# K^T and V^T of each attention head by DMA transposes in place of TensorE transposes

## The chip, the cores and the metric

The kernel runs on one core of a Trainium2 chip. The metric is device time in microseconds (us), the median of several executions. A core has TensorE (PE in the profile; its weight loads are PEld), VectorE (DVE), ScalarE (ACT), GpSimd (POOL) and SyncE (SP). In this kernel SP issues all DMA transposes, and POOL issues the ordinary loads and stores of the attention stage.

## The reference

Forward and backward pass of an attention block over a given K and V cache, multiplied by a gated branch. Cut to what the change touches (x is 2048 x 576, 32 heads of 128, 2048 keys, all bf16):

```python
q      = (xn @ wq).reshape(B, Sq, H, Dh).transpose(0, 2, 1, 3)
scores = einsum("bhqd,bhkd->bhqk", q, k_cache) * Dh ** -0.5
p      = softmax(scores)
o      = einsum("bhqk,bhkd->bhqd", p, v_cache)
s      = o.transpose(0, 2, 1, 3).reshape(B, Sq, H * Dh) @ wo
out    = x + s * silu(gated(xn))      # and the gradients of everything, by jax.vjp
```

The backward pass needs `dP = dO V^T` and `dQ = dS K`. So each head uses K and V in two forms: as they lie (keys on the partitions) for `P V` and `dS K`, and transposed (head dimension on the partitions) for `Q K^T` and `dO V^T`.

## The kernel before

Each head has two halves of 16 slots, one for each block of 128 queries. In the first half a slot makes `sp = Q K^T` and `Pq = exp(sp)`; in the second `dp = dO V^T`, and `Pq` becomes dS. Each finished 128 x 2048 slab of `Pq` (512 KB) is turned by a DMA transpose on SP's queue, into `PT` or `dST`, and TensorE reads that five slots later (`SKEW`), as weights of the "tail" matmuls. So 32 slabs per head already went through the DMA transpose.

```python
def pe_transpose_blocks(src_fn, lo, hi, dst_fn, eng):
    for g in range(lo, hi, 8):
        n = min(8, hi - g)
        pt = acc_tile(bf)
        for j in range(n):
            nc.tensor.transpose(pt[:, j, :], src_fn(g + j), ident[:])
        alt.copy(dst_fn(g, n), pt[:, :n, :], eng=eng)
...
def prep_kt(hs):      # 16 TensorE transposes, two ACT copies out of PSUM
    KTv = hs.KT[:].rearrange("p (t q) -> p t q", q=P)
    pe_transpose_blocks(lambda j: hs.Kn[:, j, :], 0, NT, lambda g, n: KTv[:, g:g + n, :], "s")

def prep_vt(hs):      # 16 TensorE transposes, two DVE copies out of PSUM
    VTv = hs.VT[:].rearrange("p (t q) -> p t q", q=P)
    pe_transpose_blocks(lambda j: hs.Vn[:, j, :], 0, NT, lambda g, n: VTv[:, g:g + n, :], "v")
...
def transpose_slab(hs, qt, name):
    T = wpt.tile([P, NT, P], bf, name=name, tag="PT")        # 7 buffers for PT and dST together
    nc.sync.dma_start_transpose(T[:], hs.slabs[qt][:])
    return T
...
def tail_part(hs, T, rhs, part):
    ...
    for kt in range(part * NT // 2, (part + 1) * NT // 2):
        nc.tensor.matmul(hs.acc[:, 0, :], lhsT=T[:, kt, :], rhs=rhs[:, kt, :], start=(kt == 0), stop=(kt == NT - 1))
...
def plan(h):                                   # put(slot, TensorE columns, work)
    b1, b2 = 2 * NT * h, 2 * NT * h + NT       # first and second half
    pl = b2 - 2 * NT if h else None            # second half of the head before
    if h:
        ...
        for c in range(4):
            put(pl + q(c), 0, lambda c=c: load_k(hd(), c, 4))
            put(pl + q(skew + 3 + c), 0, lambda c=c: load_v(hd(), c, 4))
        ...
        put(pl + q(skew + 3), NT * P, lambda: prep_kt(hd()))
    ...
    put(b1 + q(NSC + 2), NT * P, lambda: prep_vt(hd()))
```

KT and VT have one buffer each, Kn has two, Vn has one. The slot in `put` gives the order in which work is recorded; a scheduler then moves an instruction earlier on its engine's queue when it expects it to be ready.

Of the kernel before, what the change touches and what calls it, by code (L numbers as in the profile page):

```python
# [13 lines left out]
P = 128  # L14
# [52 lines left out]
def kernel(  # L67
# [6 lines left out]
    nc = tc.nc  # L74
# [6 lines left out]
    NT = S // P  # L81
# [59 lines left out]
# [7 lines that stand above are left out]
# [4 lines left out]
    def new_head(h):  # L152
        hs = HeadState()
        hs.h = h
        hs.wq, hs.woT = wqs[h % 2], woTs[h % 2]
        hs.Kn = Kns[h % 2]
        hs.Vn, hs.VT, hs.KT, hs.QT, hs.dOT, hs.dOn, hs.Qn = Vn, VT, KT, QT, dOT, dOn, Qn
        return hs

    def load_wq(hs):  # L160
        hcols = slice(hs.h * P, (hs.h + 1) * P)
        nf = DT - 1 if KPAD else DT
        if nf:
            nc.gpsimd.dma_start(hs.wq[:, :nf, :], A_wq[:nf * P, hcols].rearrange("(i p) c -> p i c", p=P))
        if KPAD:
            nc.gpsimd.dma_start(hs.wq[LO:, nf, :], A_wq[nf * P:, hcols])

    def load_wo(hs):
        nf = (DT - 1) * P if KPAD else D
        rows = slice(hs.h * P, (hs.h + 1) * P)  # L170
        if nf:
            nc.gpsimd.dma_start(wo_h[:, :nf], A_wo[rows, :nf])
        if KPAD:
            nc.gpsimd.dma_start(wo_h[:, nf + LO:], A_wo[rows, nf:])
# [5 lines left out]
    def load_k(hs, c=0, n=1):  # L180
        load_kv(hs, hs.Kn, A_k_cache, c, n)

    def load_v(hs, c=0, n=1):
        load_kv(hs, hs.Vn, A_v_cache, c, n)
# [9 lines left out]
    def prep_kt(hs):  # L194
        KTv = hs.KT[:].rearrange("p (t q) -> p t q", q=P)
        pe_transpose_blocks(lambda j: hs.Kn[:, j, :], 0, NT, lambda g, n: KTv[:, g:g + n, :], "s")

    def prep_vt(hs):
        VTv = hs.VT[:].rearrange("p (t q) -> p t q", q=P)
        pe_transpose_blocks(lambda j: hs.Vn[:, j, :], 0, NT, lambda g, n: VTv[:, g:g + n, :], "v")  # L200

    def prep_wot(hs):
        pt = acc_tile(bf)
        for i in range(DT):
            nc.tensor.transpose(pt[:, i, :], wo_h[:, i * P:(i + 1) * P], ident[:])
        alt.copy(hs.woT[:], pt[:, :DT, :], eng="s")
# [9 lines left out]
    def prep_qt(hs, sc):  # L216
        gen_T(hs.wq, xnT, hs.QT, sc, "s")

    def prep_dot(hs, sc):
        gen_T(hs.woT, dsT, hs.dOT, sc, "v")  # L220

    def prep_don(hs, sc):
        pe_transpose_blocks(lambda j: hs.dOT[:, j * P:(j + 1) * P], sc * nb, (sc + 1) * nb,
                            lambda g, n: hs.dOn[:, g:g + n, :], "v")

    def prep_qn(hs):
        pe_transpose_blocks(lambda j: hs.QT[:, j * P:(j + 1) * P], 0, NT, lambda g, n: hs.Qn[:, g:g + n, :], "v")
# [359 lines left out]
    NSC = S // CH  # L587
    nb = CH // P

    def attention(fast):  # L590
        with ExitStack() as es:
# [9 lines left out]
            skew = min(SKEW if fast else 2, NT // 2)  # L601
# [4 lines left out]
                return ps_acc.tile([P, 8, P], bf, name="acct", tag="acc")  # L606
            acc_box[0] = acc_alloc

            def start_head(h):
                hs = heads_pre[h] if h == 0 else new_head(h)  # L610
                hs.rs_all = hstat.tile([P, NT], f32, name="rs_all")
                hs.rinv_all = hstat.tile([P, NT], f32, name="rinv_all")
                hs.negdelta = hstat.tile([P, NT], f32, name="negdelta")
                hs.rsc = hstat.tile([P, NT], f32, name="rsc")
                hs.slabs = [None] * NT
                hs.PT = [None] * NT
                hs.dST = [None] * NT
                return hs
# [41 lines left out]
            def scale_don(hs, qt):  # L660
                nc.vector.tensor_scalar(hs.dOn[:, qt, :], hs.dOn[:, qt, :], hs.rinv_all[:, qt:qt + 1], None, op0=ALU.mult)

            def scale_qn(hs, qt):
                nc.vector.tensor_scalar(hs.Qn[:, qt, :], hs.Qn[:, qt, :], hs.rinv_all[:, qt:qt + 1], None, op0=ALU.mult)
# [12 lines left out]
            def tail1(hs, qt, part):  # L677
                tail_part(hs, hs.PT[qt], hs.Vn, part)
                if part == 0:
                    return  # L680
                hs.PT[qt] = None
                op_ = hs.acc
                if qt % G4 == 0:
                    hs.o_n = stg.tile([P, G4, P], bf, name="o_n")
                alt.scaled(hs.o_n[:, qt % G4, :], op_[:, 0, :], hs.rinv_all[:, qt:qt + 1], eng=("s" if qt >= NT - skew else "v"))
                junk = wt.tile([P, P], f32, name="junk")
                nc.vector.scalar_tensor_tensor(junk[:], op_[:, 0, :], -1.0, hs.dOn[:, qt, :], op0=ALU.mult, op1=ALU.mult,  # L687
                                               accum_out=hs.negdelta[:, qt:qt + 1])
                store_nat(hs, hs.o_n, qt, on2_d)

            def post1(hs):
                nc.vector.tensor_scalar(hs.rsc[:], hs.rinv_all[:], SCALE, None, op0=ALU.mult)
# [57 lines left out]
            def part_tile():  # L750
                return stg.tile([P, NT, P], f32, name="part", tag="part", bufs=1)
# [4 lines left out]
            def put(slot, cols, fn):  # L756
                units.setdefault(slot, []).append((cols, fn))
# [18 lines left out]
            def q(k):  # L776
                return min(k, NT - 1)

            def plan(h):
                b1, b2 = 2 * NT * h, 2 * NT * h + NT  # L780
                hd = lambda: heads[h]
                pl = b2 - 2 * NT if h else None
                if h:
                    put(pl, 0, lambda: heads.__setitem__(h, start_head(h)))
                    for c in range(4):
                        put(pl + q(c), 0, lambda c=c: load_k(hd(), c, 4))
                        put(pl + q(skew + 3 + c), 0, lambda c=c: load_v(hd(), c, 4))
                    put(pl + q(4), 0, lambda: load_wo(hd()))
                    put(pl + q(5), 0, lambda: load_wq(hd()))
                    put(pl + q(skew + 3), NT * P, lambda: prep_kt(hd()))  # L790
                    put(pl + q(skew + 4), DT * P, lambda: prep_wot(hd()))
                    for sc in range(NSC):
                        put(pl + q(skew + 4 + 2 * sc), DT * CH, lambda sc=sc: prep_qt(hd(), sc))
                for qt in range(NT):
                    put(b1 + qt + skew, NT * P // 2, lambda qt=qt: tail1(hd(), qt, 0))
                    put(b1 + qt + skew, NT * P // 2, lambda qt=qt: tail1(hd(), qt, 1))
                for sc in range(NSC):
                    put(b1 + q(sc), DT * CH, lambda sc=sc: prep_dot(hd(), sc))
                    put(b1 + q(sc + 1), nb * P, lambda sc=sc: prep_don(hd(), sc))
                for qt in range(NT):  # L800
                    put(b1 + max(qt + 1, q(2 + qt // nb)), 0, lambda qt=qt: scale_don(hd(), qt))
                put(b1 + q(NSC + 2), NT * P, lambda: prep_vt(hd()))
                put(b1 + q(NTH + 2), NT * P, lambda: prep_qn(hd()))
                for qt in range(NT):
                    put(max(b1 + qt + 1, b1 + NT - 4 + qt // 2 if qt < NTH else b1 + NT + qt), 0, lambda qt=qt: scale_qn(hd(), qt))
                put(b2 + 1, 0, lambda: post1(hd()))
                parts = {}

                def first(key, rhs, lo, hi, eng, factor=1.0):
                    parts[key] = part_tile()  # L810
                    return Partial(hd(), lo, hi, rhs, parts[key], None, eng, factor)
                spread(b1 + NTH, lambda: first("v", hd().dOn, 0, NTH, "v"))
                spread(b2, lambda: Partial(hd(), NTH, NT, hd().dOn, parts["v"], out_3[0, h], None))
                spread(b2 + NTH, lambda: first("k", hd().Qn, 0, NTH, "s", SCALE))
                spread(b2 + NT, lambda: Partial(hd(), NTH, NT, hd().Qn, parts["k"], out_2[0, h], None, SCALE))
                for qt in range(NT):
                    put(b2 + qt + skew, NT * P // 2, lambda qt=qt: tail2(hd(), qt, 0))
                    put(b2 + qt + skew, NT * P // 2, lambda qt=qt: tail2(hd(), qt, 1))
# [386 lines left out]
```

## Time and profile before

| | |
|---|---|
| median of 3 runs | 5043.2 us (5036.47 to 5043.98) |
| attention stage (first sp to last dp matmul) | 490 to 3633 us: 3142 us |
| busy in it | PE 3074 us (98%), ACT 2129 us (68%), DVE 1988 us (63%) |
| one head, from its first sp matmul to that of the next | 97.68 us |

From the page of the kernel before: part 1 (busy us of each engine, share of the span, instructions), the first line of the chain that ended last, and the DMA queue that SP feeds (packets, MB, share).

```profile
PE 4922.4 (97%) x53584; PEld 3474.9 (69%) x54480; DVE 2581.2 (51%) x6705; ACT 2574.1 (51%) x4636; POOL 950.4 (19%) x1481
...
q1 hardware_dynamic: 2659746, 699.38, 75.0%
...
PE 89%; issue 4%; DMA 3%; DVE 2%; ACT 1%; POOL 0%; SPq 0%; POOLq 0%; ACTq 0%; DVEq 0%
```

TensorE is the limit. The groups of instructions of the kernel before that matter here (line, engine, operation, out<-in, shapes, count | busy us, mean ns | idle us just before them and who ended it):

```profile
L675 PE MATMUL acc<-Kn,dST 128*128 128x128 bf16 x8192 | 551.3, 219 | 10.1 <-DMA dST<-Pq 6.5
L675 PE MATMUL acc<-Vn,PT 128*128 128x128 bf16 x8192 | 548.4, 219 | 26.6 <-DMA PT<-Pq 19.6 <-issue 0.2
...
L40 ACT COPY KQ<-acct 128x1024 bf16<-128x1024 bf16 x62 | 59.7, 1015 | 15.8 <-PE acct L146 15.8
...
L42 DVE COPY VT<-acct 128x1024 bf16<-128x1024 bf16 x64 | 43.0, 683 | 0.0
L146 PE MATMUL acct<-ident,Vn 128*128 128x128 bf16 x512 | 34.1, 219 | 0.0
...
L146 PE MATMUL acct<-ident,Kn 128*128 128x128 bf16 x496 | 32.8, 219 | 1.6
```

The last two lines are what the change takes away. What 16 of them cost in the stream is read from the timeline (start us, duration us, engine, instruction); here the 16 for K in one head, the ACT copies that empty them, and the dp matmuls that follow:

```profile
2022.18 1.09 PEld L146 LDWEIGHTS <-Kn 128*128 128x128 bf16 x16
2022.40 1.06 PE L146 MATMUL acct<-ident,Kn 128*128 128x128 bf16 x16
...
2023.04 1.93 ACT L40 COPY KQ<-acct 128x1024 bf16<-128x1024 bf16 x2 [0.51 <-PE acct L146]
...
2023.29 0.59 PE L698 MATMUL dp<-VT,dOT 128*128 128x512 bf16 x2
```

The next matmul starts 0.89 us after the first transpose, so 16 transposes hold the stream for 0.89 us, although the last one's modelled end comes at 1.06 us.

The view of the tile dST of the kernel before gives the slab transposes (issue time in ns, min/median/max), how long TensorE's matmuls and weight loads sat idle for a slab (us, times; both rows of TensorE counted, so some of it twice), and the time from issue to landing:

```profile
L622 SPq DMA_TRANSPOSE dST<-Pq x512: 1417/2229/7093, 536.0 to 3636.7; - x171
...
  DMA dST<-Pq: 15.1, 19
...
DMA to landing us min/median/max: 3.6/5.2/11.3
```

### The profile page before, as it was taken

To read this page: it belongs to the slowest core of one execution; us is meant where nothing else is said; L and a number is where in the kernel's file an instruction comes from. 1 tells how busy PE (TensorE), PEld (TensorE's weight loads), DVE (VectorE), ACT (ScalarE), POOL (GpSimd) and SP (SyncE) were. 2 spreads that over 40 slices of the span, in tenths; PEclk is the share of its full clock that TensorE was granted. 3 is DMA by queue.
4 is the path that set the end of the run, shared out by engine and by line. 5 is a ranking of instruction groups with operands and counts; after the bars stand their busy time and mean duration, and the time that the engine had idled before them with its cause. 6 is when DMAs were issued, how large, how long until landed. Compare 5 with 4: busy or idle time off the path is not lost.

```text
span 5053.4 us, 128161 instructions
## 1 busy us (share of the span) xinstructions
PE 4922.4 (97%) x53584; PEld 3474.9 (69%) x54480; DVE 2581.2 (51%) x6705; ACT 2574.1 (51%) x4636; POOL 950.4 (19%) x1481
## 2 busy tenths in 40 slices
PE   8999999999999999999999999999789999999999
PEld 3445777777777787777778777777646666555554
DVE  4544666666566666666656666665425444200111
ACT  4432766666666676666667666666313333211000
POOL 3322111111111111111111111111122222211000
PEclk9999999999999999999999999999999999999999
DMA  7886999999999999999999999999996665797976
GB/s 249 271 202 171 212 208 211 203 211 209 207 214 214 201 212 207 210 205 211 214 202 209 215 206 207 208 213 202 197 201 204 193 183 181 213 266 187 173 141 121
DMA packets 2762675, 1031.39 MB, mean 204 GB/s; under 512 B 2665249, under 2 KB 2669474, under 8 KB 2762082
## 3 DMA queue, kind: packets, MB, share of 16 engines
q1 hardware_dynamic: 2659746, 699.38, 75.0%
q0 software_dynamic: 101728, 323.05, 20.1%
q8 instruction: 428, 7.01, 0.6%
q14 instruction: 165, 1.35, 0.1%
q10 hardware_dynamic: 608, 0.59, 0.0%
HBM read 175.31 MB, written 182.13 MB: 71 GB/s over the span
## 4 chain that ended last, share of the span: by engine, by line
PE 89%; issue 4%; DMA 3%; DVE 2%; ACT 1%; POOL 0%; SPq 0%; POOLq 0%; ACTq 0%; DVEq 0%
PE acc L734 17%; PE acc L675 17%; PE acc L960 13%; PE sp L628 7%; PE acc L1131 7%; PE dp L698 7%; PE acc L213 6%; PE g_ps L446 3%; PE u_ps L448 3%; PE dh L1013 3%; PE acc L531 2%; PE acct L146 2%; PE acc L930 2%; DMA dST<-Pq 1%; DVE Pq L701 1%
## 5 line engine op out<-in xcount | busy, mean ns | idle before, releaser
L646 ACT ACTIVATE Pq<-sp 128x1024 bf16<-128x1024 f32 x1024 | 1047.1, 1023 | 330.4 <-PE sp L628 199.1
L734 PEld LDWEIGHTS <-Pq 128*128 128x128 bf16 x16384 | 1002.9, 98 | 240.5 <-issue 1.1
L705 ACT ACTIVATE t<-dp,negdelta 128x1024 bf16<-128x1024 f32 x512 | 571.1, 1116 | 222.6 <-PE dp L698 169.0
L701 DVE SCALAR_TENSOR_TENSOR Pq<-dp,negdelta,Pq 128x1024 bf16<-128x1024 f32 x512 | 654.9, 1279 | 38.6 <-PE acc L675 37.5
L675 PEld LDWEIGHTS <-PT 128*128 128x128 bf16 x8192 | 503.3, 98 | 142.2 <-DMA PT<-Pq 20.9
L675 PE MATMUL acc<-Vn,PT 128*128 128x128 bf16 x8192 | 548.4, 219 | 26.6 <-DMA PT<-Pq 19.6
L675 PE MATMUL acc<-Kn,dST 128*128 128x128 bf16 x8192 | 551.3, 219 | 10.1 <-DMA dST<-Pq 6.5
L734 PE MATMUL acc<-dOn,Pq 128*128 128x128 bf16 x8192 | 547.4, 219 | 10.2 <-DVE junk L687 0.2
L628 PE MATMUL sp<-KQ 128*128 128x512 bf16 x1762 | 548.4, 380 | 2.6 <-ACT Pq L646 2.4
L698 PE MATMUL dp<-VT,dOT 128*128 128x512 bf16 x1728 | 540.0, 379 | 7.6 <-DVE Pq L701 7.6
L734 PE MATMUL acc<-Qn,Pq 128*128 128x128 bf16 x8192 | 540.6, 219 | 3.4
L706 DVE TENSOR_TENSOR Pq<-t,Pq 128x1024 bf16<-128x1024 bf16 x512 | 354.3, 692 | 365.8 <-ACT t L705 359.0
L675 PEld LDWEIGHTS <-dST 128*128 128x128 bf16 x8192 | 492.0, 98 | 69.5 <-DMA dST<-Pq 8.6
L715 ACT ACTIVATE dq_n<-acc,rsc 128x128 bf16<-128x128 f32 x512 | 188.1, 367 | 333.0 <-PE acc L675 331.9
L1147 DVE SCALAR_TENSOR_TENSOR junk<-acc,xn_all 128x512 f32<-128x512 f32 (+1 forms) x32 | 13.9, 453 | 637.0 <-ACT dxn L1146 637.0
L748 POOL DMA_DIRECT2D out_dram<-kvo x256 | 140.2, 548 | 1019.0 <-DVE kvo L746 1011.0
L669 POOL DMA_DIRECT2D on_d<-o_n x128 | 97.0, 758 | 750.7 <-DVE junk L687 396.7
L1015 DVE TENSOR_TENSOR du_blk<-dh,ah 128x256 bf16<-128x256 f32 x288 | 120.1, 417 | 191.6 <-PE dh L1013 189.5
L50 DVE TENSOR_SCALAR o_n<-acc,rinv_all 128x128 bf16<-128x128 f32 x352 | 123.2, 350 | 180.9 <-PE acc L675 180.9
L1146 ACT ACTIVATE dxn<-acc 128x512 f32<-128x512 f32 (+1 forms) x32 | 12.8, 406 | 393.6 <-PE acc L1131 386.2
L633 DVE TENSOR_REDUCE rs_all<-rsp 128x1 f32<-128x2 f32 x512 | 78.0, 152 | 256.3 <-ACT Pq L646 254.1
L646 ACT ACTIVATION_READ_ACCUMULATOR Pq<-sp 128x1 f32 x1024 | 200.4, 196 | 0.0
(206 smaller groups left out, 6949.9 us busy)
## 6 DMA issues: line engine op xcount, KB each, us to landing
out_dram<-kvo POOLq DMA_DIRECT2D x256, 128.0 KB, 4.2
ah<-a_d POOLq DMA_DIRECT2D x18, 1024.0 KB, 7.1
ah<-h_d POOLq DMA_DIRECT2D x18, 1024.0 KB, 9.5
du_d<-du_blk POOLq DMA_DIRECT2D x18, 1024.0 KB, 8.1
dg_d<-dg_blk POOLq DMA_DIRECT2D x18, 1024.0 KB, 9.9
h_d<-h_row POOLq DMA_DIRECT2D x64, 256.0 KB, 3.5
a_d<-a_row POOLq DMA_DIRECT2D x64, 256.0 KB, 3.7
x_all<-in_A_k_cache_dram SPq DMA_DIRECT2D x64, 256.0 KB, 4.0
```

The lines of the kernel that those rows point to most:

```text
L213: nc.tensor.matmul(av[:, :CH], lhsT=w[:, i, :], rhs=srcT[:, i, cs], start=(i == 0), stop=(i == DT - 1))
L628: nc.tensor.matmul(sp[:, c * CH:(c + 1) * CH], lhsT=hs.QT[:, qt * P:(qt + 1) * P], rhs=hs.KT[:, hf * HW_ + c * CH: hf * HW_ + (c + 1) * CH ...
L646: nc.scalar.activation(Pq[:, hsl], sp[:], AF.Exp, scale=SCALE, accum_out=hs.rsp[:, hf:hf + 1])
L675: nc.tensor.matmul(hs.acc[:, 0, :], lhsT=T[:, kt, :], rhs=rhs[:, kt, :], start=(kt == 0), stop=(kt == NT - 1))
L698: nc.tensor.matmul(dp[:, c * CH:(c + 1) * CH], lhsT=hs.dOT[:, qt * P:(qt + 1) * P], rhs=hs.VT[:, hf * HW_ + c * CH: hf * HW_ + (c + 1) * C ...
L701: nc.vector.scalar_tensor_tensor(Pq[:, hsl], dp[:], hs.negdelta[:, qt:qt + 1], Pq[:, hsl], op0=ALU.add, op1=ALU.mult)
L705: nc.scalar.activation(t[:], dp[:], AF.Identity, bias=hs.negdelta[:, qt:qt + 1], scale=1.0)
L706: nc.vector.tensor_tensor(Pq[:, hsl], t[:], Pq[:, hsl], op=ALU.mult)
L715: nc.scalar.activation(hs.dq_n[:, qt % G4, :], hs.acc[:, 0, :], AF.Copy, scale=hs.rsc[:, qt:qt + 1])
L734: nc.tensor.matmul(self.tile[:, j, :], lhsT=self.slabs[qt][:, kt * P:(kt + 1) * P], rhs=self.rhs[:, qt, :], start=(qt == self.lo), stop=(q ...
L960: nc.tensor.matmul(accs[j][:, :nn], lhsT=lhs[:, st, cols], rhs=rhs[:, st, n0:n0 + nn], start=(st == 0), stop=(st == NT - 1))
L1131: nc.tensor.matmul(self.accs[sl][j][:, :nn], lhsT=ch[:, kk, sl * P:(sl + 1) * P], rhs=wT[:, k0 + kk, n0:n0 + nn], start=(self.k + kk == 0) ...
```

## The change

The DMA transpose can read Kn and Vn where they lie. The intent is to take 1008 transposes from the engine that is the limit, with their PSUM copies, and to give 63 more transposes of 512 KB to a queue that already does 1024 of them. Head 0's K^T is made before the attention stage and stays as it was.

```diff
+            def turn_nat(dst, src):
+                nc.sync.dma_start_transpose(dst[:].rearrange("p (t q) -> p t q", q=P), src[:].rearrange("p t d -> p (t d)"))
+
...
-                    put(pl + q(skew + 3), NT * P, lambda: prep_kt(hd()))
+                    put(pl + q(skew + 3), 0, lambda: turn_nat(hd().KT, hd().Kn))
...
-                put(b1 + q(NSC + 2), NT * P, lambda: prep_vt(hd()))
+                put(b1 + q(NSC + 2), 0, lambda: turn_nat(hd().VT, hd().Vn))
```

In the built program the K^T transpose of the next head stands on SP's queue just before the last P slab of a head. V^T stands just before the last dS slab.

## The prediction

> **What bounds it now.** TensorE. The page gives PE 97% busy of 5053.4 us, and the chain of waits is 89% PE. The change touches the attention stage (490 to 3640 us, 32 heads). In its windows of 100 us PE is busy 98.7, DVE 64, ACT 68; the clock is 1.00. In the timeline the first sp matmul of a head follows that of the head before after 97.68 us, nearly always the same: a stream bound by PE's own work. PE waits for PT or dST transposes only 26 us in the whole run (groups of instructions: 19.6 + 6.5).
>
> **What goes.** Per head, 16 transposes each of Kn and Vn on PE (31 heads for K, since head 0's is made before attention and stays; 32 for V): 1008 matmuls. The groups give them 32.8 us (496) and 34.1 us (512), 67 us together, but count the pipelined end of each run of 16. By timeline and chain the stream moves on 0.89 us per 16 (2022.40 to 2023.29, 2070.20 to 2071.09). So PE gains 63 x 0.89 = 56 us at least, 67 at most. The Trainium skill ("TensorE: Matmul & The Clock Gate", Part 4: PE-mode transpose) gives about 275 ns for one in a kernel; this trace shows 56 ns in a run, which I use. Also gone: 62 ACT copies of 1.015 us and 64 DVE copies of 0.683 us (63 + 44 us). Both engines have a third of their time free; I count nothing for those.
>
> **What comes.** 63 DMA transposes of 512 KB on the SP queue beside 1024 of the same shape: +6%. Those take 2.1 to 2.2 us of SP's time to issue (median) and 4.9 to 5.2 us to land; one goes out every 3.05 us. The DMAs have room, though not much: 205 GB/s on average with peaks near 300 in single slices. The skill ("DMA: Bandwidth & Descriptors", Latency and other measured facts) gives 261 GB/s for DMA transposes; an estimate from it is 2.0 us for each, 4 us more per head of about 96.
>
> **What moves.** In the built program V^T stands just before a head's last dS transpose, so it can go once the last dp matmul has read the old V^T; K^T stands just before the last P transpose. Each is wanted half a head (48 us) later. Those places are slack: slabs at the end of a phase land 6 to 11 us before PE reads them, while slabs 3 to 7 have 2 to 4 us. So a few landings slip by 2 us and PE waits little. PE's order is otherwise nearly unchanged.
>
> **On the critical path:** all of the 56 us, minus up to some 10 us of new waits for slabs, plus perhaps a few us because copies no longer stand before exp and t.
>
> **Predicted time: 4988 us (-1.1%), 80% range 4970 to 5012.** Faster by over 2%: 0.04; within 2%: 0.90; slower by over 2%: 0.06.
>
> **What would show it.** Head period falls from 97.68 to about 95.9 us; PE busy falls by about 60 us, ACT by 63, DVE by 44; groups with ident,Kn and ident,Vn are gone (but 16); PE waits for PT and dST stay under 40 us; the SP queue moves some 33 MB more; later stages keep their lengths.
>
> **What would make it wrong.** If SP's queue is nearer to full than its average tells (from 2013 to 2025 us it issues back to back, 3 to 4 us each, beside loads and stores), one more transpose pushes the train back and PE waits at slabs 3 to 6: 2 us per phase would eat everything (64 x 2 = 128 us, +1.4%). If ACT or DVE set the pace in slots that lose PE work, part of the gain goes unused.

## The result, and the profile after

| | before | after |
|---|---|---|
| median | 5043.59 us of 4 runs (5036.47 to 5046.36) | 5033.67 us of 4 runs (5021.17 to 5043.95) |
| ratio after to before | | 0.9981, 95% interval 0.9956 to 1.0006 |
| span of the profiled run | 5053.4 us | 5031.3 us |
| attention stage in it | 3142 us | 3114 us |

The result counts as the same, about 10 us less. The predicted time, 4988 us with a range from 4970, was missed: the measured one lies above the range's upper end of 5012 us.

The same lines of the page of the changed kernel:

```profile
PE 4871.2 (97%) x52577; PEld 3418.4 (68%) x53472; DVE 2548.0 (51%) x6641; ACT 2520.7 (50%) x4574; POOL 950.6 (19%) x1481
...
q1 hardware_dynamic: 2790786, 732.42, 81.0%
...
PE 85%; DMA 7%; issue 5%; DVE 2%; ACT 1%; POOL 1%; SPq 0%; POOLq 0%; ACTq 0%; DVEq 0%
```

PE is 51 us less busy, ACT 53, DVE 33, and 33.04 MB more pass SP's queue. But DMA now stands in the chain with 7% where it had 3%. The groups that answer to those of before (ident,Kn and ident,Vn have gone):

```profile
L678 PE MATMUL acc<-Kn,dST 128*128 128x128 bf16 x8192 | 557.3, 219 | 34.2 <-DMA dST<-Pq 28.9
L678 PE MATMUL acc<-Vn,PT 128*128 128x128 bf16 x8192 | 543.0, 219 | 25.2 <-DMA PT<-Pq 18.3 <-issue 0.2
```

And the tile view of dST of the changed kernel:

```profile
L625 SPq DMA_TRANSPOSE dST<-Pq x512: 1418/2375/7496, 540.1 to 3609.8; - x171
...
  DMA dST<-Pq: 67.3, 69
...
DMA to landing us min/median/max: 3.8/5.5/11.9
```

The waits for P slabs are what they were; those for dS slabs rose from 19 to 69 times. So the place to look at is the second half of a head. Worked out from the starts of the sp and dp matmuls in both traces: the shortest head is 97.68 us before and 95.90 us after, a difference of exactly 2 x 0.89. Among heads 1 to 30 the first half of a head was nearly always 48.50 us (before 49.40). The second half was 47.39 us at best (before 48.29), but longer than that by more than 0.3 us in 20 of 31 heads, against 4 before. The sum of that excess for heads 1 to 30 is 33.4 us; before it was 3.6.

The longest of these stalls in the timeline of the changed kernel (lines of several short windows, in order of time; the first DVE line finishes slab 0 of dS, the second slab 2):

```profile
2956.02 1.84 SPq L610 DMA_TRANSPOSE KQ<-Kn  x1
2957.34 1.28 DVE L704 SCALAR_TENSOR_TENSOR Pq<-dp,negdelta,Pq 128x1024 bf16<-128x1024 f32 x1
2957.95 4.40 SPq L625 DMA_TRANSPOSE PT<-Pq  x1
2962.44 1.58 SPq L625 DMA_TRANSPOSE dST<-Pq  x1
2962.59 1.28 DVE L704 SCALAR_TENSOR_TENSOR Pq<-dp,negdelta,Pq 128x1024 bf16<-128x1024 f32 x1
2964.12 2.55 SPq L625 DMA_TRANSPOSE dST<-Pq  x1
2966.41 1.63 POOL L178 DMA_DIRECT2D Vn<-in_A_v_cache_dram  x3 [1.10 <-PE acc L678]
2966.76 3.92 SPq L625 DMA_TRANSPOSE dST<-Pq  x1
2968.78 0.54 POOL L178 DMA_DIRECT2D Vn<-in_A_v_cache_dram  x1
2970.77 7.33 SPq L625 DMA_TRANSPOSE dST<-Pq  x1
2978.39 1.47 PEld L678 LDWEIGHTS <-dST 128*128 128x128 bf16 x16 [3.28 <-DMA dST<-Pq]
2978.40 1.73 PE L678 MATMUL acc<-Kn,dST 128*128 128x128 bf16 x16 [2.79 <-DMA dST<-Pq]
```

Slab 0 is ready at 2958.62 (2957.34 + 1.28) and issued at 2962.44, because the K^T transpose and the last P slab stand before it. Slab 2 is ready at 2963.87, issued at 2966.76, just when POOL issues the four loads of the next head's V, and lands at 2978.39. TensorE waited 2.79 us for it. The 7.33 us of the next slab is not a wait for data: the Trainium skill ("Perfetto Trace Analysis", DMA Instruction — HWDGE (DVE, Sync)) says that such an instruction's profiled start is when all its semaphores are satisfied and that its end is when the sequencer is free again. The trace agrees insofar as that slab was ready at 2966.52, by the DVE, long before its issue at 2970.77.

From all heads, medians in us (worked out from the traces; "late" is from the slab's last write to the start of its issue, "landing" from there to its landing, "spare" from landing to TensorE's first weight load of it; 0.04 spare means that TensorE was waiting; 24 to 32 of 32 landings could be matched):

| slab of the second half | before: late, landing, spare | after: late, landing, spare |
|---|---|---|
| 2 | 0.03, 4.62, 6.48 | 2.02, 7.31, 2.19 |
| 3 | 0.03, 8.60, 1.92 | 2.40, 8.33, 0.04 |
| 4 | 0.64, 8.47, 2.46 | 3.85, 6.74, 0.61 |
| 5 | 2.98, 6.19, 3.65 | 5.57, 5.51, 2.32 |

Slabs 3 and 4 already had little to spare before. Now every slab at the start of the second half is issued 2 to 3 us later, and slab 3 is typically just too late. By slab, TensorE's matmuls in heads 0 to 30 of the profiled run waited 10.0 us for slab 2 (8 times), 11.9 for slab 3 (16 times) and 5.3 for slab 4 (5 times); before, all dS slabs of these heads cost 2.3 us. All issues of these transposes together, summed from the trace, take 2471 of the 3142 us before (79%) and 2826 of 3114 us after (91%).

### The profile page after: what moved, and what is told of

Read it like the earlier page. It is cut to its first block, busy times and chain, and to the rows that moved or that the text cites. A ratio compares the mean times of both kernels' runs of the same rounds, so it can differ in the third digit from the quotient of the medians.

```text
span 5031.3 us, 126205 instructions
## 1 busy us (share of the span) xinstructions
PE 4871.2 (97%) x52577; PEld 3418.4 (68%) x53472; DVE 2548.0 (51%) x6641; ACT 2520.7 (50%) x4574; POOL 950.6 (19%) x1481
## 4 chain that ended last, share of the span: by engine, by line
PE 85%; DMA 7%; issue 5%; DVE 2%; ACT 1%; POOL 1%; SPq 0%; POOLq 0%; ACTq 0%; DVEq 0%
PE acc L737 16%; PE acc L678 16%; PE acc L963 13%; PE sp L631 7%; PE acc L1134 7%; PE dp L701 6%; PE acc L213 6%; DMA dST<-Pq 4%; PE g_ps L446 3%; PE u_ps L448 3%; PE dh L1016 3%; PE acc L531 2%; PE acc L933 2%; PE acct L146 1%; DMA PT<-Pq 1%
## 5 line engine op out<-in xcount | busy, mean ns | idle before, releaser
L649 ACT ACTIVATE Pq<-sp 128x1024 bf16<-128x1024 f32 x1024 | 1047.0, 1024 | 295.8 <-PE sp L631 181.8
L678 PE MATMUL acc<-Kn,dST 128*128 128x128 bf16 x8192 | 557.3, 219 | 34.2 <-DMA dST<-Pq 28.9
L678 PE MATMUL acc<-Vn,PT 128*128 128x128 bf16 x8192 | 543.0, 219 | 25.2 <-DMA PT<-Pq 18.3
```

Source lines behind the costliest of these rows:

```text
L649: nc.scalar.activation(Pq[:, hsl], sp[:], AF.Exp, scale=SCALE, accum_out=hs.rsp[:, hf:hf + 1])
```

## The experiments

The theories: **P** (place): the K^T transpose stands just ahead of a run of slabs that has little to spare, and delays it; V^T's place costs nothing. **L** (load): the queue and the DMAs are nearly full, so any added transpose costs alike. **C** (pace): ACT or DVE set the pace in the freed slots, so the freed time can't be used. The second batch tests place and slack. The third sets a **collision** theory (the V loads make slabs 3 and 4 slow) against a **backlog** theory (only the queue behind K^T counts), and the fourth holds the controls. Every timed kernel had 4 to 6 runs, and the kernel before 11 in each batch, on the same chip as its batch. Diffs are against the changed kernel unless said otherwise.

All results (saved = (1 - ratio) x the median of before in that batch; the last two columns are worked out from each one's profiled run: time of heads 1 to 30, and what their second halves lost against the shortest one):

| run | median us | ratio (95% interval) | saved us | heads 1-30 us | lost in second halves us |
|---|---|---|---|---|---|
| before | 5042 to 5049 by batch | 1 | 0 | 2934.0 | 3.6 |
| after | 5033.67 | 0.9981 (0.9956 to 1.0006) | 10 | 2910.8 | 33.4 |
| e1_no_turn | 4996.87 | 0.9901 (0.9885 to 0.9917) | 50 | 2886.5 | 8.2 |
| e2_v_only | 5029.90 | 0.9973 (0.9959 to 0.9987) | 14 | 2909.1 | 4.4 |
| e3_k_only | 5042.55 | 0.9992 (0.9977 to 1.0008) | 4 | 2934.1 | 29.1 |
| e4_both_same | 5072.09 | 1.0050 (1.0033 to 1.0067) | -25 | 2947.5 | 17.0 |
| e5_k_late | 5012.55 | 0.9944 (0.9930 to 0.9959) | 28 | 2897.7 | 17.1 |
| e6_k_tight | 5024.92 | 0.9967 (0.9955 to 0.9980) | 17 | 2901.2 | 22.7 |
| e7_after_skew6 | 5006.20 | 0.9921 (0.9908 to 0.9934) | 40 | 2896.6 | 13.8 |
| e8_before_skew6 | 5039.77 | 0.9994 (0.9982 to 1.0007) | 3 | 2939.6 | 0.1 |
| e9_vload_late | 5005.65 | 0.9918 (0.9901 to 0.9934) | 41 | 2883.3 | 1.6 |
| e10_klate_vload | 5022.16 | 0.9950 (0.9935 to 0.9966) | 25 | 2903.3 | 20.7 |
| e11_klate_skew6 | 5004.78 | 0.9918 (0.9901 to 0.9935) | 41 | 2895.0 | 8.5 |
| e12_klate_vload_skew6 | 5029.82 | 0.9960 (0.9940 to 0.9981) | 20 | 2928.8 | 32.4 |
| e13_before_vload | 5043.10 | 0.9994 (0.9980 to 1.0007) | 3 | 2931.8 | 0.1 |
| e14_kvload_late | 5027.05 | 0.9966 (0.9947 to 0.9985) | 17 | 2898.9 | 21.1 |
| e15_vload_skew6 | 4998.86 | 0.9902 (0.9883 to 0.9921) | 49 | 2899.3 | 3.4 |
| e16_no_turn_vload | 4993.40 | 0.9900 (0.9883 to 0.9917) | 50 | 2877.2 | 0.1 |

A profiled run is one sample, and runs of one kernel spread by 10 to 40 us. So use the ratios, and the last two columns tell where the time went. They are to be read with care: the profiled run of e9 was the fastest of its six, those of e12 and e15 were the slowest of theirs, and that of the kernel before was 12 us above its median. Neither column holds the last head, which took 109 to 130 us from one profiled run to another.

### First batch: is the time freed, and which transpose costs it?

**e1: neither kind of transpose.** K^T and V^T stay those of head 0; the result is wrong.

```diff
-                    put(pl + q(skew + 3), 0, lambda: turn_nat(hd().KT, hd().Kn))
+                    pass
...
-                put(b1 + q(NSC + 2), 0, lambda: turn_nat(hd().VT, hd().Vn))
+                if h == 0:
+                    put(b1 + q(NSC + 2), 0, lambda: turn_nat(hd().VT, hd().Vn))
```

> Neither PE transposes nor DMA transposes of K and V after head 0 (K^T and V^T stay those of head 0, so the result is wrong on purpose). If PE's freed time is usable (place theory P and load theory L both say so), all head periods are 95.90 us, PE idles on dST no more than before (some 9 us in attention), and the time is about 4983 us (-1.2%). If ACT or DVE set the pace of the freed slots (theory C), periods stay above 96.5 us and the time is above 5010.

50 us are saved, somewhat less than the 56 to 60 that were expected, but the interval (42 to 58 us) holds 56. The median head is 95.90 us. So C falls: TensorE can use the freed time. In the changed kernel about 40 of these 50 us came back.

**e2: V^T alone by DMA.** K^T by TensorE as before.

```diff
-                    put(pl + q(skew + 3), 0, lambda: turn_nat(hd().KT, hd().Kn))
+                    put(pl + q(skew + 3), NT * P, lambda: prep_kt(hd()))
```

> V^T by DMA, K^T on PE as before. P (K^T's place just ahead of the dS train is what costs; V^T's place is free): head periods 96.79 us with few longer ones, 5043 - 28 = about 5015 us. L (any added transpose costs alike because the DMAs are nearly full): half of the gain and half of the loss, about 5038.

**e3: K^T alone by DMA.** V^T by TensorE as before.

```diff
-                put(b1 + q(NSC + 2), 0, lambda: turn_nat(hd().VT, hd().Vn))
+                put(b1 + q(NSC + 2), NT * P, lambda: prep_vt(hd()))
```

> K^T by DMA, V^T on PE. P: best head period 96.79 us but many longer, all of the new wait on dST (about +25 us of PE idle in attention), so 5035 to 5050 us, no gain. L: the same as for V alone, about 5038.

The tile view of dST, the idle time of TensorE for a slab, first with V^T alone (e2), then with K^T alone (e3):

```profile
  DMA dST<-Pq: 11.2, 21
```

```profile
  DMA dST<-Pq: 64.0, 58
```

K^T alone brings nearly all of the new waits (64.0 of the 67.3 us of the changed kernel) and saves nothing that is clear of noise. V^T alone brings none: its heads 1 to 30 are 24.9 us shorter than before, near the 27 us (30 x 0.89) that were freed. So by the waits it is P. By time V^T alone saved 14 us (7 to 21), half of what P expected; what takes the rest is not seen in heads 1 to 30, and it stays open. Part of it may be noise of the last head: it took 119.8 us in the profiled run of e2, and 110.8 in that of e1; one profile of each can't show more.

**e4: both kinds at once.** The DMA transposes in the same places, and then the TensorE transposes over the same bytes.

```diff
                     put(pl + q(skew + 3), 0, lambda: turn_nat(hd().KT, hd().Kn))
+                    put(pl + q(skew + 3), NT * P, lambda: prep_kt(hd()))
...
                 put(b1 + q(NSC + 2), 0, lambda: turn_nat(hd().VT, hd().Vn))
+                put(b1 + q(NSC + 2), NT * P, lambda: prep_vt(hd()))
```

> The cost by itself: K^T and V^T by DMA in the places of the changed kernel, and afterwards the PE transposes and copies as before, over the same bytes. P and L: before plus the new waits on dST alone, about 5043 + 30 = 5065 to 5090 us, or a little less because the head has 1.8 us more for the same transfers. C: the same as before, 5043.

25 us slower than before. This is the cost of the transposes by themselves, on a TensorE that is slower by 1.8 us per head. On the faster TensorE of the changed kernel it is 40 us (after against e1).

### Second batch: place and slack

**e5: K^T further back on the queue,** behind the 13th dS slab of the head before; `issue_after` only sets the order on SP's queue.

```diff
-                nc.sync.dma_start_transpose(T[:], hs.slabs[qt][:])
+                hs.turned = nc.sync.dma_start_transpose(T[:], hs.slabs[qt][:])
...
-                    put(pl + q(skew + 3), 0, lambda: turn_nat(hd().KT, hd().Kn))
+                    def kt_late():
+                        with tc.issue_after(heads[h - 1].turned.ins):
+                            turn_nat(hd().KT, hd().Kn)
+                    put(pl + q(12), 0, kt_late)
```

> The changed kernel with the K^T transpose queued behind the 13th dS transpose of the head before (two slots before the V^T transpose), where slabs land 7 us or more before PE reads them. P: nearly all head periods 95.90 us, PE idle on dST back to some 10 us, about 4988 us (-1.1%). L: as the changed kernel, about 5033.

Same work, same bytes, other place: 28 us saved in place of 10, and the two intervals barely touch (0.9956 to 1.0006 and 0.9930 to 0.9959). L alone can't explain that, and the waits for dS slabs fall from 67.3 to 23.9 us (tile view). The slabs at the start of the second half are again issued without delay (late 0.03 us at slab 3, 0.61 at slab 4). But P expected more. TensorE's matmuls still waited 7.8 us for slabs 3 and 4, and there is a new wait: the first sp matmul of the next head now waits for K^T itself. The waits of PE name it:

```profile
PE sp L631 <- DMA KQ<-Kn: 5.4, 6, 2.1
```

**e6: K^T in the middle of the late slabs,** behind the 5th dS slab: as e5, with `put(pl + q(4), 0, kt_late)`.

> The changed kernel with the K^T transpose queued behind the 5th dS transpose, in the middle of the late slabs. P: worse than the changed kernel, nearly every head period longer than 96.5 us, 5040 to 5080 us. L: as the changed kernel, about 5033.

This was a miss: 17 us saved, so not worse than the changed kernel but, if anything, better. The same figures as in the table of slabs, worked out for this run (16 to 24 of 32 landings matched), suggest why. Slabs 3 and 4 are issued in time again (late 0.03 and 0.19 us). Slabs 5 and 6 are now issued 6.14 and 6.39 us late and land 0.74 and 0.25 us before use, where before they had 3.65 and 3.83 us. TensorE's waits move from slabs 2 to 4 to slabs 4 to 6 (6.0, 7.6 and 3.7 us). An entry ahead of a whole run of slabs delays all of them; one in the middle spares the tightest and spends what the later ones have. P was too simple: what counts is the tightest slab behind the entry, not how busy the queue is at the entry.

**e7 and e8: one slot more of slack,** in the changed kernel and, as a control, in the kernel before.

```diff
-    SKEW = 5
+    SKEW = 6
...
-            wpt = pool("wpt", 7 if fast else 4)
+            wpt = pool("wpt", 8 if fast else 4)
...
-                            fo_ = stg.tile([P, 4, P], bf, name="kvo", bufs=4)
+                            fo_ = stg.tile([P, 4, P], bf, name="kvo", bufs=3)
```

> The changed kernel, tails one slot later (SKEW 6, 8 slab buffers in place of 7; one kvo buffer less to make room). The same transposes in the same places but 2.65 us more slack. P and L, where L means lateness only: the stalls vanish, periods 95.90, about 4990 us. If the DMAs were over capacity, more slack would not help: about 5033.

> Control: the kernel before with SKEW 6, 8 slab buffers and one kvo buffer less. It hardly waited for slabs, so 5030 to 5043 us; only a few us from the rare stalls at slabs 3 to 6.

The changed kernel saves 40 us with it, the kernel before 3 (no difference clear of noise). This is less than the 4990 us that were expected: the stalls shrank but did not vanish (13.8 us in second halves; the tile view of dST has 34.8 us in place of 67.3). Still, what was lost was mostly lateness of slabs, not throughput of the DMAs: the same bytes pass in a shorter time.

### Third batch: what makes slabs 3 and 4 slow?

In the kernel before, too, slabs 3 and 4 took over 8 us to land where the median slab takes 5.2. In the timeline POOL's four V loads of 128 KB fall there.

**e9: the V loads eight slots later,** behind the second dq store; K^T stays where the change put it.

```diff
+            stored = [None]
+
+            def v_late(hs, c):
+                with tc.issue_after(stored[0].ins):
+                    load_v(hs, c, 4)
...
-                    nc.gpsimd.dma_start(dst_d[...], buf[:])            # the o and dq stores
+                    stored[0] = nc.gpsimd.dma_start(dst_d[...], buf[:])
...
-                        put(pl + q(skew + 3 + c), 0, lambda c=c: load_v(hd(), c, 4))
+                        put(pl + q(13), 0, lambda c=c: v_late(hd(), c))
```

> The changed kernel with the four loads of the next head's V moved from slots 4 and 5 of the second half of a head to slot 12 (behind the second dq store); the K^T transpose stays just ahead of the dS train. If the V loads are what makes slabs dST 3 and 4 take 7 to 8 us to land (collision theory), their landing falls to about 5 us, the loss in the second halves of heads 1 to 30 falls from 33 us to under 12, and the time is 5000 to 5012 us. If the queue's own backlog behind the K^T transpose is all (backlog theory), landings of dST 3 and 4 stay at 7 us or more and the time stays about 5033.

41 us saved, of the 50 that e1 shows to be there. Landings of slabs 3 and 4 fall from 8.33 and 6.74 us to 6.03 and 5.85 (medians), though these slabs are still issued about 2 us late. They have 2.54 and 2.70 us to spare (16 of 32 landings could be matched here). The tile view of dST in e9:

```profile
L631 SPq DMA_TRANSPOSE dST<-Pq x512: 1422/2336/5698, 538.7 to 3578.0; - x171
...
  DMA dST<-Pq: 11.1, 11
...
DMA to landing us min/median/max: 3.6/5.6/10.1
```

The median landing did not fall, 5.6 us against 5.5. The queue is as full as before (issues take 2807 of 3082 us, 91%). The stalls in second halves are gone from this run (the fastest of the six) because the slow landings no longer meet the slabs without slack. So it takes both: the backlog behind K^T and the collision with the V loads. Backlog alone falls, since e9 left the backlog in place.

**e10: e5 and e9 together.**

> Both: K^T behind the 13th dS transpose and the V loads at slot 12. Collision theory: no stall in the second halves, heads at 95.90 us, 4995 to 5003 us. Backlog theory: as K^T late alone, about 5013; slower if the loads now collide with the K^T and V^T transposes.

A miss: 25 us, clearly less than e9 alone and no more than e5 alone (28). dS slabs no longer wait (the tile view has 3.2 us), but now the V loads at slot 12 collide with the K^T transpose at slot 13, which takes 6.84 us to land (median; 5.46 in e5), and the next head waits for it. From the tile view of KQ (idle time of TensorE for K^T) and one such case in the timeline of e10:

```profile
  DMA KQ<-Kn: 47.3, 28
```

```profile
2505.40 2.13 POOL L178 DMA_DIRECT2D Vn<-in_A_v_cache_dram  x4
...
2508.49 5.64 SPq L610 DMA_TRANSPOSE KQ<-Kn  x1
...
2517.75 1.03 PE L637 MATMUL sp<-KQ 128*128 128x512 bf16 x2 [3.25 <-DMA KQ<-Kn]
```

**e11: e5 and e7 together. e12: e5, e7 and e9 together.**

> K^T late and tails one slot later (8 slab buffers, one kvo buffer less). Slack and place add: 4995 to 5003 us. If the queue is simply full, as skew 6 alone, 5006.

> All three. Nothing of the slabs can be late any more: as without the transposes, 4990 to 4998 us, the best of all.

e11 saves 41 us, no more than e7 alone (40). e12 saves only 20 where the best of all was expected. The collision of e10 is in it: the waits of PE for K^T are the longest of all, 30.7 us in the profiled run, the slowest of its six (by the same view e10 has 19.8).

```profile
PE sp L637 <- DMA KQ<-Kn: 30.7, 10, 5.7
```

### Fourth batch: controls

**e13: the kernel before with the V loads late** (the edit of e9 on the kernel before).

> Control: the kernel before, V loads at slot 12 of the second half. It lost only 3.6 us in its second halves, so if the gain of e9 is the collision with the added K^T transpose, this is within 6 us of before, about 5038 to 5045. If the V loads cost something by themselves, it gains 15 us or more, below 5030.

3 us, nothing clear of noise. So the V loads cost the kernel before nothing that can be seen in its time, and e9's gain belongs to their meeting with the change. The run also shows without any added transpose that these loads are what slows the two slabs: with the loads moved, slabs 3 and 4 land after 5.61 and 5.88 us (medians), where the kernel before had 8.60 and 8.47; it had slack enough to hide this.

**e14: e9 with the K loads late too,** behind the on store of slot 12 of the first half.

```diff
+            def k_late(hs, after, c):
+                with tc.issue_after(after.ins):
+                    load_k(hs, c, 4)
...
-                        put(pl + q(c), 0, lambda c=c: load_k(hd(), c, 4))
+                        put(pl + q(c), 0, lambda c=c: k_late(hd(), heads[h - 1].on7, c))
```

> The changed kernel with the V loads late and the K loads late too (slot 12 of the first half in place of slots 4 and 5). If the K loads delay P slabs 4 and 5 as the V loads delay dS slabs 3 and 4, their landing falls from 7 to 8 us to about 5; first halves lost only 0.2 us per head, so the time stays about 5000 to 5006. If K^T now waits for its load and holds up the queue, above 5015.

17 us saved, against 41 for e9, so it is worse, as its last sentence allowed, but by another way: K^T does not wait for its load, which had landed at least 1.5 us before it was issued. P slabs 4 and 5 do land sooner (5.45 and 5.40 us, 7.82 and 6.74 in the changed kernel). But slabs 12 and 13 now take 8.45 and 7.09, the last P slab is 6.01 us late, and the delay runs on into the dS slabs.

**e15: e9 and e7 together.**

> The changed kernel, V loads late, SKEW 6 with 8 slab buffers and one kvo buffer less, K^T where the change put it. If lateness of slabs is all that is left, 4993 to 5002. If it is not, as e9, 5006, or worse as e12 was.

49 us saved: the best of all that give the right result, but its interval overlaps that of e9. Both beat the kernel before and the changed one; neither by over 2%.

**e16: e1 with the V loads late,** the floor for this placement. Its output is wrong, which doesn't matter for the time.

> No transposes of K and V at all after head 0 (wrong on purpose) and the V loads late: the floor for this placement. If the two transposes cost nothing any more in e9, this is the same as e9 within 5 us; the difference to e9 is what they still cost. I expect 4990 to 4997.

50 us saved, with heads of 95.89 to 96.17 us without exception. Compared with e9 (5005.65 us) the transposes still cost about 9 us by the ratios (0.9918 and 0.9900), which is within the intervals. In the two profiled runs e9's heads 1 to 30 are 6.1 us longer, most of it in first halves, where TensorE waited 4.4 us for P slabs.

## Why the prediction was wrong

- **What bounds it, and what goes: right.** The head fell from 97.68 to 95.90 us where nothing stalled, as predicted to 0.1 us, and e1 shows 50 us of usable time where 56 were forecast. PE busy fell by 51 us (60 foreseen), ACT by 53 (63), DVE by 33 (44).
- **What comes: right in bytes, useless in kind.** 33.04 MB more passed, as said. "The DMAs have room" held on average: e9 moved the same bytes and saved 41 us. The estimate of 2.0 us for each from the skill's 261 GB/s ("DMA: Bandwidth & Descriptors") was near the median issue of K^T, 2.01 us, but V^T took 2.91 us and they landed after 5 to 6 us. The average told nothing of the stalls.
- **What moves: here the step failed.** The prediction said "Those places are slack: slabs at the end of a phase land 6 to 11 us before PE reads them, while slabs 3 to 7 have 2 to 4 us. So a few landings slip by 2 us and PE waits little." It had both figures, but it judged the entry by the spare time of the slab next to it and did not carry the delay along the queue to the slabs behind. K^T stood before the last P slab, which had 6 us; but slabs 3 and 4 of dS, four and five places further back, had 1.92 and 2.46 us, and were now issued 2.4 and 3.2 us later. A slot of the second half (2.65 us in the timeline) leaves the queue little time to catch up. So PE's waits for dS slabs rose from 6.5 to 28.9 us.
- **The term that was mis-sized:** "minus up to some 10 us of new waits for slabs" was 40 us by time (after 10 saved, e1 50, each with its interval); in the profiled runs the second halves show 30 of it (33.4 us lost against 3.6). The check set for it, waits for PT and dST under 40 us, came out at 47 us (18.3 + 28.9).
- **The warning had it:** the prediction's own "one more transpose pushes the train back and PE waits at slabs 3 to 6" is what happened, at slabs 2 to 4, in about two heads of three, and nearly only in second halves. It was given too small a chance. What it lacked was the partner, the V loads at the same slots, although it had seen "beside loads and stores" in the trace.
- **Later stages** were 1426.7 us against 1420.6 in the profiled runs; in the other profiles they range from 1412.9 to 1424.6, so an effect of the change is not shown. All kernels also have one stall of up to 20 us in the last head, when wo is loaded.

What stays open: why V^T alone saves 14 us by time where its heads show 25, and the part of the last 9 us between e9 and e16 that its heads do not show. By which part of the DMA path a load slows a transpose beside it was not tried.

## What to carry to other kernels

Before adding an entry to an in-order queue, list for every later entry how long before its use it lands, and look at the smallest, not at the entry's neighbour and not at the queue's average. When work is moved off a bound engine, that engine also consumes faster, so the slack of what feeds it shrinks together with the gain (here the same transposes cost 25 us in e4, with the slower TensorE, and 40 in the changed kernel; the intervals of the two costs overlap). If the gain does not come, look for what else moves at the tight place: here shifting four loads by eight slots raised the saving from 10 to 41 of 50 us, while two fixes that worked alone (e5 28 us, e9 41) saved 25 together (e10).

## What the Trainium skill lacked or had wrong

- "TensorE: Matmul & The Clock Gate", Part 4: PE-mode transpose, gives about 275 ns for a transpose in a kernel and says that the full clock doesn't engage for it. It doesn't say how transposes in a run overlap: here one is 219 ns long in the profile, but 16 in a run held the stream 0.89 us, 56 ns each. The granted clock was 1.00 there; ordinary matmuls stand on both sides, so this doesn't test what transposes alone would get.
- "DMA: Bandwidth & Descriptors" has a bandwidth for DMA transposes, 261 GB/s, and for earlier generations a count of sequencer cycles by tiles, but no time for which an SBUF-to-SBUF one of a given size holds the issuing queue beside other traffic: for the dS slabs 512 KB took 1.42 us at least, 2.2 us in the median of the kernel before and 2.4 us after, up to 7.5 us, and landed after 3.6 to 11.9 us.
- The same page, Rules for kernel authors, says that a transpose next to ordinary DMAs needs nothing. That is about correctness, and every run that was meant to give the right result did. No page has a figure for what they cost in time: beside four loads of 128 KB from POOL, slabs 3 and 4 took 8.3 and 6.7 us to land; with the loads moved, 6.0 and 5.9 us.
- No page tells how to read a DMA share of the profile (the time that packets took, as a share of 16 engines) above 1; in the attention stage it was 1.08 before and 1.17 after, while PE was busy 98 and 97% of the stage.
- "TensorE: Matmul & The Clock Gate", Part 1, states that the clock is halved after an idle window of about 3.4 us. In the stall shown above PE was idle for less, 2.79 us by its modelled ends, and then the granted clock was 0.5 for 3.41 us, from 2978.60. A stall of 2.65 us in another head, at 2195.34, was followed by no such stretch. So the length of the halved stretch is like that of the page's window, but less idle time was enough here. The head lost 4.81 us in its second half, with PE idle for 3.2 us in all, so this stall cost more than its own length. The window of the changed kernel (busy us and counts of each engine, clock, DMA share, GB/s):

```profile
2970.00:2985.00 15.00, 11.93 (x144) 9.55 (x144) 8.65 (x10) 5.83 (x8) 2.39 (x4) 0.89 1.28 186
```
